# Wide queries, 129-column key-value products, split key weights, and tile keys that are spread without transfers, in a four-layer attention kernel

## The chip, the cores and the metric

The kernel runs on one core of a Trainium2 chip. The core has five engines that run their own instruction streams and wait for each other through semaphores: TensorE (PE, matrix products into PSUM, with PEld for its weight loads), VectorE (DVE), ScalarE (ACT), GpSimd (POOL) and SyncE (SP), which here only issues transfers. Sixteen DMA engines move data. The metric is the device time of one execution in microseconds, less is better, as a median over several runs.

## The reference: what is computed

A stream `x` of 2048 tokens by 512 values (bfloat16) passes through four residual layers. Layers 1 and 3 are linear attention (A), layers 2 and 4 are attention over a sliding window of 256 tokens (B); both have 32 heads of 16 values.

```
phi = lambda t: jnp.where(t > 0, t + 1, jnp.exp(t)) + 1e-6
pq, pk = phi(q), phi(k)
kv = jnp.einsum("bhsd,bhse->bhde", pk, v)
z = jnp.einsum("bhsd->bhd", pk)
num = jnp.einsum("bhqd,bhde->bhqe", pq, kv)
den = jnp.einsum("bhqd,bhd->bhq", pq, z)[..., None] + 1e-6
o = num / den
...
x = x + _A_ref(_layernorm(x, axis=-1), A_wqkv, A_wo)
x = x + _B_ref(_layernorm(x, axis=-1), B_wqkv, B_wo)
x = x + _A_ref(_layernorm(x, axis=-1), A_wqkv, A_wo)
x = x + _B_ref(_layernorm(x, axis=-1), B_wqkv, B_wo)
```

B is softmax attention in which token i sees tokens i-255 to i. Layer A couples all tokens: `kv` and `z` are sums over the whole sequence, so no output of layer 3 exists before the last key and value of layer 3.

## The kernel before

Tokens are worked on in 16 tiles of 128. Everything stays in SBUF; only weights, `x` and the result pass through HBM. The work falls into five stretches, and neighbouring layers overlap in them:

- **Keys of layer 1** (`layer_a_keys`): per tile the normalisation (`norm`: statistics and `xn` on DVE, a power on POOL), the transpose into `XQ` (by PE for the first five tiles, by DMA for the others), the keys `k`, their feature map `phi` (`E` on ACT, `E1` and `phi` on DVE; for some tiles `R` on ACT and `mx` on DVE in place of `phi`), and a running product of keys and normalised input (`g`, L501).
- **First barrier** (`barrier(1)`): `kv`, its masked copy `pqd`, the four products `M` with the output weights, the denominators (`den`, `rec`, `spread`, and `pqd` or `sc` with `pm`).
- **Middle of layer 2** (`middle(2)`): for each tile the end of layer 1 (`aout`, `res`, a second `norm`, transposed into `xT`), the projections of layer 2 (`bq`, `bk`, `bv`), scores, exponentials on ACT (L686, L801, L721, L754), masks on DVE and POOL, values (`pv`), the end of layer 2 and the keys and values of layer 3.
- **Second barrier** (`barrier(2)`): the same for layer 3. Here `kv` is summed from keys and values tile by tile (`a_kv`).
- **Middle of layer 4** (`middle(3)`, called the last layer here) with the write of the result.

The queries of A (`a_q`, L434 of the form ps<-XQ,wA) are not tied to a place: they fill PE wherever it would wait. One call handles a tile: two groups of eight products of 128x128 by 128 columns, then `phi` into the same columns of `XQ`.

In `a_kv` each tile takes four products of 128 columns (L477) and four of one column with a vector of ones (L480), which give `z`. The result has values on partitions and keys in columns, which is the side from which the product `M` (L547) reads it.

The denominators come from five steps of four products each; the first of the five adds the 1e-6 through a small product of constants (`eps`, `ones`).

The keys of layer B stand in `kB` in a form with every second entry zero, because 64 keys and 64 zeros are interleaved for two heads. In most tiles `bk` is evicted once (`bke`, L627 on ACT, L628 on DVE) into a zeroed buffer, from which two transfers (`kd`, L636) write the even and the odd partitions into `kB`. For tile 0 alone (`NEAR`) two evictions with a per-partition factor of one or zero (`kz`, L624) write `kB` directly. `kB` has four slots; tile t uses slot t modulo 4.

The order of the work is written out. The program lists its operations with their data dependencies; `place` reads from a packed string, `TABLE`, the order of all operations, the engine of each one that may run on two, and the PSUM bank of each tile. Each engine plays its instructions in that order, and a semaphore wait is put where a dependency crosses engines. So an instruction that waits holds up all that stand behind it on its engine. All input and transposing transfers, `kd` and `vd`, and a part of the output transfers are issued by SP in one queue.

Of the kernel before, what the change touches and what calls it, by code (L numbers as in the profile page):

```python
# [11 lines left out]
P = 128  # L12
# [3 lines left out]
T = 16  # L16
# [207 lines left out]
NEAR = (0,)  # L224
# [11 lines left out]
class Plan:  # L236
# [51 lines left out]
    def setup(self):  # L288
# [10 lines left out]
        seq += [xs(0, 1), w("wAk", "wA", "A_wqkv", 512, 1024), xs(1, 2), w("wAq", "wA", "A_wqkv", 0, 512), xs(2, 4), xs(4, 6), xs(6, 8), xs(8, 12)]  # L299
# [4 lines left out]
        for i, (n, f, b, r) in enumerate(seq):  # L304

            begun.append(self.load(n, f, b, r, key + i if i < 8 else 100.5 + 0.5 * i, begun[i - 4:i - 3] if i >= 7 else []))
# [59 lines left out]
    def norm(self, t, key, xn_slot, out, wr, by_pe, po=None, near=False):  # L366

        K = self
        xn, name = (lambda: K.vA[:, t, :], ("vA", t)) if xn_slot is None else (lambda: K.xn[:, xn_slot, :], ("xn", xn_slot))
# [40 lines left out]
    def tok(self, name, t, lhs, rhs, rd, key, whole=False):  # L410
# [5 lines left out]
        for h in range(2):  # L416
# [5 lines left out]
            self.pe(name, put, key - 0.001 * h, 2, 512, rd=rd, ps=[ps])  # L422
# [16 lines left out]
    def phi(self, ps, out, wr, key, ring, near=False):  # L439
# [3 lines left out]
        view = lambda x: x if len(out().shape) == 2 else x.rearrange("p (f n) -> p f n", f=4)  # L443
        self.on("ACT", "E", lambda e: e.activation(K.tE[:, s, :], K.ps(ps), ACT.Exp, bias=0.0), key, act(512), wr=[("tE", s)], ps=[ps])  # L444
        if near:
            self.on("ACT", "R", lambda e: e.activation(out(), view(K.ps(ps)), ACT.Identity, bias=K.one[:]), key + 0.005, act(512), rd=[("one",)], wr=wr, ps=[ps])
# [3 lines left out]
        else:  # L450
            self.on("DVE", "phi", lambda e: e.scalar_tensor_tensor(out(), view(K.ps(ps)), 1.0 + 1e-6, view(K.tE[:, s, :]), ALU.add, ALU.max), key + 0.02, dve(512), rd=[("tE", s)], wr=wr, ps=[ps])

    def a_k(self, t, key):
        K = self
        xT = lambda c: K.XQ[:, c, t * P:(t + 1) * P]
        ps = self.tok("k", t, xT, lambda c: K.wA[:, c, 512:1024], [("XQ", t), ("wAk",)], key)
        self.phi(ps, lambda: K.pk[:, t, :], [("pk", t)], key + 0.1, 0)

    def a_v(self, t, key):
# [3 lines left out]
        self.copy("ve", ps, lambda: K.vA[:, t, :], lambda: K.ps(ps), key + 0.1, 512, wr=[("vA", t)] + ([("kS", 0), ("kS", 1)] if t == 2 else []))  # L463

    def a_q(self, t, key, near=False):
        K = self
        ps = self.feat("q", t, lambda c, f: K.wA[:, c, f * P:(f + 1) * P], lambda c: K.XQ[:, c, t * P:(t + 1) * P], [("XQ", t), ("wAq",)], key)
        self.phi(ps, lambda: K.XQ[:, :, t * P:(t + 1) * P], [("XQ", t)], key + 0.1, 1, near)

    def a_kv(self, t, kv, z, key):  # L470
        K = self

        def put(e):
            m = None
            for f in range(4):
                fs = slice(f * P, (f + 1) * P)
# [692 lines left out]
```

## Time and profile before

| what | value |
|---|---|
| median of three runs | 409.82 us (409.52 to 409.96) |
| the profiled execution | 409.61 us, of which 407.9 us are the span from the first to the last instruction |
| granted TensorE clock | 1.00 |
| PE, DVE, ACT, POOL busy | 385.7, 347.8, 349.4, 131.3 us |

A busy time is the time in which at least one instruction of the engine was under way. For PE it includes the tail of some 0.17 us in which the last product of a group drains, so the rate of a product is better read from the chain of work, where a group counts only until the next one begins. A row of the chain or of the timeline has the start, the length, the engine, the tiles, the line of the program and how many instructions are in it; what stands in square brackets is the idle time of the engine ahead of it and what ended it. A row of the groups has the busy time, the mean duration of one instruction in ns, and the idle time ahead of it. Rows of the windows have, after the length, the busy time of PE, PEld, DVE, ACT and POOL with the count of instructions.

### The profile page before, as it was taken

How to read it: one execution, taken by the hardware profiler on the slowest of the kernel's cores; microseconds unless marked ns; L12 is line 12 of the kernel's file. 1: busy time of each engine (PE TensorE's matmuls, PEld its weight loads, DVE VectorE, ACT ScalarE, POOL GpSimd, SP SyncE). 2: the span in 40 equal slices, each digit the busy share in tenths (PEclk: the TensorE clock that was granted, in tenths of full speed). 3: DMA queues.
4: the chain of work that ended last, by engine and by line, in shares of the span. 5: the costliest groups of instructions: out<-in, count | busy, mean ns of one | idle time of the engine just before them, and what ended most of it. 6: DMA issues, size and time to landing. Idle time of an engine off the chain costs nothing.

```text
span 407.9 us, 17534 instructions
## 1 busy us (share of the span) xinstructions
PE 385.7 (95%) x7667; PEld 261.3 (64%) x7742; DVE 347.8 (85%) x807; ACT 349.4 (86%) x441; POOL 131.3 (32%) x221
## 2 busy tenths in 40 slices
PE   8999999998999999999999999999999989998996
PEld 3754776776575567565667677686756756666664
DVE  7998899999989999888788779998998688856865
ACT  3753679998999999999997258999999999999992
POOL 5668542211430241432512302230305234510340
PEclk9999999999999999999999999999999999999999
DMA  7567024523354444453232000344315534442551
GB/s 251 117 152 232 15 56 107 119 69 81 80 80 106 71 101 104 92 112 91 56 50 62 14 2 2 102 114 107 94 42 106 90 90 104 81 99 70 136 134 54
DMA packets 66788, 37.19 MB, mean 91 GB/s; under 512 B 47640, under 2 KB 62104, under 8 KB 66712
## 3 DMA queue, kind: packets, MB, share of 16 engines
q1 hardware_dynamic: 66320, 35.02, 36.7%
q8 instruction: 61, 1.00, 1.1%
q0 software_dynamic: 384, 1.05, 0.8%
q14 instruction: 15, 0.12, 0.1%
q10 hardware_dynamic: 8, 0.00, 0.0%
HBM read 6.29 MB, written 2.10 MB: 21 GB/s over the span
## 4 chain that ended last, share of the span: by engine, by line
PE 52%; ACT 31%; DVE 9%; issue 4%; DMA 2%; POOL 1%; POOLq 0%; DVEq 0%
ACT pb L686 20%; PE ps L420 18%; PE ps L434 15%; PE ps L822 6%; ACT vp L686 5%; PE ps L676 4%; PE ps L501 3%; ACT pb L801 3%; DVE stats L374 1%; DVE pb L694 1%; DVE xres L604 1%; ACT tE L444 1%; PE ps L792 1%; DMA XQ<-xn 1%; ACT pb L754 1%
## 5 line engine op out<-in xcount | busy, mean ns | idle before, releaser
L686 ACT ACTIVATE pb<-ps 128x1024 bf16<-128x1024 f32 (+2 forms) x216 | 199.0, 1019 | 6.2 <-PE ps L676 5.3
L822 PEld LDWEIGHTS ps<-vB,pb 128*128 128x128 bf16 x2560 | 79.0, 96 | 13.3 <-DVE pb L694 2.8
L822 PE MATMUL ps<-vB,pb 128*128 128x34 bf16 x2560 | 84.9, 177 | 0.9 <-DVE xn L381 0.5
L434 PE MATMUL ps<-xT,wBp 128*128 128x128 bf16 x1024 | 69.3, 219 | 1.3 <-DMA xT<-xn 0.8
L434 PEld LDWEIGHTS ps<-xT,wBp 128*128 128x128 bf16 x1024 | 58.9, 98 | 13.7 <-issue 4.0
L772 POOL TENSOR_SCALAR_AFFINE_SELECT pb<-pb 128x1024 bf16<-128x1024 bf16 x35 | 40.1, 1145 | 84.2 <-DVE pb L694 33.8
L379 POOL TENSOR_SCALAR ve<-mv 128x1 f32<-128x1 f32 x63 | 16.6, 264 | 149.1 <-DVE mv L375 146.9
L444 ACT ACTIVATE tE<-ps 128x512 bf16<-128x512 f32 x64 | 38.1, 606 | 25.3 <-PE ps L420 12.5
L676 PE MATMUL ps<-XQ,kB 32*128 32x256 bf16 (+3 forms) x992 | 48.0, 267 | 2.9 <-ACT vp L686 0.5
L604 DVE TENSOR_TENSOR xres<-ps,xres 128x512 bf16<-128x512 f32 x63 | 43.0, 684 | 7.3 <-PE ps L420 6.8
L420 PE MATMUL ps<-wA,XQ 128*128 128x512 bf16 x174 | 45.8, 379 | 3.4 <-DMA XQ<-xn 0.9
L694 DVE TENSOR_TENSOR pb<-pb,tri 128x512 bf16<-128x512 bf16 (+1 forms) x108 | 43.6, 417 | 2.7 <-ACT pb L686 2.0
L374 DVE BATCH_NORM_STATS2 stats<-xres 128x6 f32<-128x512 bf16 x64 | 43.5, 683 | 2.5 <-DMA xres<-in_A_x_dram 1.9
L380 POOL TENSOR_TENSOR rs<-ve,negh 128x1 f32<-128x1 f32 x64 | 39.5, 616 | 7.7 <-DVE ve L377 2.4
L801 ACT ACTIVATE pb<-ps 128x1024 bf16<-128x1024 f32 x42 | 41.3, 1058 | 0.5 <-PE ps L792 0.4
L434 PE MATMUL ps<-XQ,wA 128*128 128x128 bf16 x512 | 35.5, 219 | 0.2 <-issue 0.2
L434 PEld LDWEIGHTS ps<-XQ,wA 128*128 128x128 bf16 x512 | 30.8, 98 | 6.6 <-DVE xres L604 0.2
L420 PE MATMUL ps<-wBv,xT 128*128 128x512 bf16 x107 | 30.6, 380 | 2.8 <-issue 1.6
L420 PE MATMUL ps<-M,XQ 128*128 128x512 bf16 x112 | 30.5, 380 | 2.0 <-DVE XQ L591 0.5
L420 PE MATMUL ps<-wBo,oT 128*128 128x512 bf16 x109 | 29.8, 380 | 1.8 <-issue 0.8
L676 PEld LDWEIGHTS ps<-XQ,kB 32*128 32x128 bf16 x992 | 14.9, 92 | 25.7 <-ACT pb L686 8.4
L834 DVE RECIPROCAL rc<-ps 128x16 f32<-128x16 f32 x64 | 16.2, 253 | 14.4 <-PE ps L822 13.9
(126 smaller groups left out, 557.4 us busy)
## 6 DMA issues: line engine op xcount, KB each, us to landing
vB<-vS SPq DMA_DIRECT2D x64, 136.0 KB, 2.5
kB<-vp SPq DMA_DIRECT2D x60, 128.0 KB, 2.2
wA<-in_A_wqkv_dram SPq DMA_DIRECT2D x3, 512.0 KB, 4.5
xres<-in_A_x_dram SPq DMA_DIRECT2D x2, 512.0 KB, 5.6
pb<-in_B_wqkv_dram SPq DMA_DIRECT2D x1, 1024.0 KB, 5.5
out_dram<-xres POOLq DMA_DIRECT2D x8, 128.0 KB, 3.2
out_dram<-xres SPq DMA_DIRECT2D x7, 128.0 KB, 3.0
xres<-in_A_x_dram SPq DMA_DIRECT2D x3, 256.0 KB, 4.8
```

The lines of the kernel that those rows point to most:

```text
L374: self.on("DVE", "stats", lambda e: e.bn_stats(K.stats[:, t, :], x()), key, dve(512), rd=rd, wr=[("stats", t)], **held)
L380: self.pow = self.on("POOL", "pow", lambda e: e.tensor_tensor(K.rs[:, t, :], K.ve[:, t, :], K.negh[:], ALU.pow), key + 0.03, (640, 690), r ...
L420: m = e.matmul(K.ps(ps), lhs(c), rhs(c), start=c == 0 and not whole, stop=c == 3)
L434: m = e.matmul(K.ps(ps)[:, f * P:(f + 1) * P], w(c, f), xT(c), start=c == 0, stop=c == 3)
L444: self.on("ACT", "E", lambda e: e.activation(K.tE[:, s, :], K.ps(ps), ACT.Exp, bias=0.0), key, act(512), wr=[("tE", s)], ps=[ps])
L604: self.on("DVE", "res", lambda e: e.tensor_tensor(K.xres[:, t, :], K.ps(po), K.xres[:, t, :], ALU.add), key, dve(512), rd=[("xres", t)], w ...
L676: m = e.matmul(K.ps(ps[gq])[:, ns * i:ns * i + ns], K.kB[rows, j % 4, 2 * f + b, :, :], K.XQ[rows, f, q:q + ns], start=True, stop=True, ti ...
L686: return e.activation(out(2 * h, 2, ns), i, ACT.Exp, bias=0.0, scale=0.25)
L694: return e.tensor_tensor(x, x, K.tri[:, 0, sh:64].unsqueeze(1).unsqueeze(1).to_broadcast([P, 4, n, 64 - sh]), ALU.mult)
L772: return e.affine_select(out=x, in_=x, compare_op=ALU.is_ge, fill=0.0, base=-2, pattern=[[0, 16], [-2, 64]], channel_multiplier=1)
L801: return e.activation(far(h), i, ACT.Exp, bias=0.0, scale=0.25)
L822: m = e.matmul(K.ps(ps)[:, 34 * u:34 * u + 34], K.P((b // 2) % rp)[:, gq, f, o:o + P], K.vB[:, (b // 2) % 4, b % 2, r, :], start=i == 0, s ...
```

## The change

Five edits and a new table:

1. **Wide queries.** `a_q` handles a pair of tiles: each of the two PSUM tiles takes two of the four feature blocks, with products of 256 columns that span both tiles. Per pair that is 16 products of 256 columns for 32 of 128. The feature map then writes two feature blocks of both tiles, and may do so only when everything that reads the two tiles of `XQ` has been done.
2. **129-column key-value products.** The rows of `vA` grow from 512 to 516 columns; behind every 128 columns of values stands a one, written by `unit`, two POOL instructions in all. `a_kv` takes four products of 129 columns, whose last column is `z`; the products with the vector of ones are gone. Keys now lie on partitions, so the masked `kv` goes through four PE transposes and a copy before `M`. `kvm` and `zs` become two halves each. The rows of `vA` in layer 1, from which the transposing transfers read, start at multiples of 1032 bytes, where it was 1024.
3. **Denominators.** For the last three of four groups the product with the constants goes, and a DVE instruction `de` adds 1e-6 in PSUM.
4. **Split key weights.** The key weights arrive in two transfers of 256 KB, and each half of the first product waits for its own.
5. **Keys of tiles 8 to 15 of the last layer** take the path of tile 0: two evictions `kz`, no `bke`, no `kd`.

The new `TABLE`, unpacked, has 2564 operations for 2559. By engine, before and after: PE 866 and 867, ACT 440 and 441, DVE 806 and 820, POOL 217 and 220, SP 230 and 216. All 16 new `kz` stand on DVE, as the eight `bke` in their place did. The copy of the transposed `kv` stands on DVE. Of the masks `mf` of layer 2, five move from DVE to POOL and one the other way before its last tiles. In the second barrier the transposed `xn` of the last tile is evicted by DVE in place of ACT, three queries' steps (two `E`, one `R`) stand ahead of the first eviction of `xT`, and one eviction of `xT` moves from ACT to DVE. On SP the output of one early tile stands behind the two last halves of the result. Otherwise the new order resembles the old one, with neighbours exchanged.

```diff
-NEAR = (0,)
+NEAR = {2: (0,), 3: (0, 8, 9, 10, 11, 12, 13, 14, 15)}
...
+        def wk(h):
+            return ("wAk%d" % h, lambda e: e.dma_start(K.wA[:, 2 * h:2 * h + 2, 512:1024], K.A_wqkv.rearrange("(k p) c -> p k c", p=P)[:, 2 * h:2 * h + 2, 512:1024]), 262144, [("wAk", h)])
...
-        self.copy("ve", ps, lambda: K.vA[:, t, :], lambda: K.ps(ps), key + 0.1, 512, wr=[("vA", t)] + ([("kS", 0), ("kS", 1)] if t == 2 else []))
...
+    def a_q(self, u, keys, near):
...
+        own = [("XQ", 2 * u), ("XQ", 2 * u + 1)]
+        wide = lambda t: slice(256 * (t // 2), 256 * (t // 2) + 256)
...
+                    f = 2 * (t % 2) + h
+                    for c in range(4):
+                        m = e.matmul(K.ps(ps)[:, 256 * h:256 * h + 256], K.wA[:, c, f * P:(f + 1) * P], xT(c), start=c == 0, stop=c == 3)
...
+        held = [o for x in own for o in self.g.r[x]]
...
+            self.phi(tiles[d], out, wr, keys[d] + 0.1, 1, t in near, after=held)
+
+    def unit(self, a, b, more, key):
...
+        self.g.add("unit", {"POOL": (300, 360), "DVE": dve(4 * (b - a))}, lambda e, eng: e.memset(x(), 1.0), key, wr=[("vA", t) for t in range(a, b)] + more)
...
-                e.matmul(K.ps(kv)[:, fs], K.vA[:, t, fs], K.pk[:, t, fs], start=t == 0 and f == 0, stop=t == T - 1, skip_group_check=True)
...
-                m = e.matmul(K.ps(z)[:, f:f + 1], K.pk[:, t, fs], K.ones[:, 0:1], start=t == 0 and f == 0, stop=t == T - 1, skip_group_check=True)
+                m = e.matmul(K.ps((kv, z)[f // 2])[:, 129 * (f % 2):129 * (f % 2) + 129], K.pk[:, t, f * P:(f + 1) * P], K.vA[:, t, 129 * f:129 * f + 129], start=t == 0 and f % 2 == 0, stop=t == T - 1, skip_group_check=True)
...
+        if late:
+            for h, x in enumerate((kv, z)):
...
+                self.on("DVE", "kvm", lambda e, h=h, two=two: e.tensor_tensor(K.oT[:, 0, 2 * h:2 * h + 2, :], two()[:, :, 0:P], K.bmask[:].unsqueeze(1).to_broadcast([P, 2, P]), ALU.mult), key - 2, dve(256), rd=[("bmask",)], wr=[("kvT", h)] + ([] if h else [("oT", 0)]), ps=[x])
...
+            self.transpose("T", lambda: K.oT[:, 0, :, :].rearrange("p f n -> p (f n)"), lambda: K.pqd[:], [("oT", 0), ("kvT", 0), ("kvT", 1)], [("pqd",)], key - 2, True)
...
-                for i in range(5):
+                for i in range(1 if G else 0, 5):
...
+            if G:
+                self.on("DVE", "de", lambda e, ps=ps: e.tensor_scalar(K.ps(ps)[:, 0:P], K.ps(ps)[:, 0:P], 1e-6, None, op0=ALU.add), k + 0.05, dve(128), ps=[ps])
...
-        if t in NEAR:
+        if t in NEAR[2 + (self.rp == 4)]:
...
+ROW = D + 4
...
-            sb("vp", [2 * T, D]); sb("kB", [4, 8, 64, 2]); sb("vB", [4, 2, 16, 34]); sb("pb", [3, 4, 4, 704])
+            sb("vp", [T * (ROW + D)]); sb("kB", [4, 8, 64, 2]); sb("vB", [4, 2, 16, 34]); sb("pb", [3, 4, 4, 704])
```

More of the change, by code (lines that the diff above doesn't have):

```diff
@@ L437, in feat, with phi @@
         return ps
-    def phi(self, ps, out, wr, key, ring, near=False):
+    def phi(self, ps, out, wr, key, ring, near=False, after=()):
         K = self
@@ L450, in phi @@
         else:
[L451 removed]
+            self.on("DVE", "phi", lambda e: e.scalar_tensor_tensor(out(), view(K.ps(ps)), 1.0 + 1e-6, view(K.tE[:, s, :]), ALU.add, ALU.max), key + 0.02, dve(512), rd=[("tE", s)], wr=wr, ps=[ps], after=after)
     def a_k(self, t, key):
@@ L949, in middle @@
         if not last:
+            self.unit(0, LATE, [("kS", 0), ("kS", 1)], base + 14)
             for j in range(LATE):
```

178 lines of the change are left out of this document (98 added, 80 removed).

## The prediction

> **What bounds the kernel now.** I read the page first for the engines and the chain of work, then the busy time by stretches, then the chain piece by piece where the change touches it.
>
> ```profile
> PE 385.7 (95%) x7667; PEld 261.3 (64%) x7742; DVE 347.8 (85%) x807; ACT 349.4 (86%) x441; POOL 131.3 (32%) x221
> ...
> PE 52%; ACT 31%; DVE 9%; issue 4%; DMA 2%; POOL 1%; POOLq 0%; DVEq 0%
> ```
>
> PE holds half of the chain and ACT a third, so the bound changes from stretch to stretch. The windows show where (columns: length, then PE, PEld, DVE, ACT, POOL busy):
>
> ```profile
> 7.00:57.00 50.00, 49.45 (x522) 30.33 (x527) 46.37 (x115) 28.09 (x50) 32.57 (x63) 1.00 0.49 130
> 57.00:90.00 33.00, 31.90 (x614) 23.43 (x610) 30.83 (x71) 31.63 (x39) 7.76 (x18) 1.00 0.41 101
> 90.00:117.00 27.00, 24.62 (x555) 16.79 (x557) 26.68 (x63) 25.52 (x31) 8.70 (x12) 1.00 0.41 80
> 117.00:213.00 96.00, 92.12 (x1895) 60.11 (x1917) 83.08 (x193) 94.13 (x109) 28.61 (x45) 1.00 0.40 86
> 213.00:249.00 36.00, 34.36 (x622) 25.59 (x629) 29.07 (x68) 20.38 (x37) 6.90 (x11) 1.00 0.12 25
> 249.00:276.00 27.00, 26.69 (x504) 19.90 (x507) 26.55 (x63) 25.68 (x35) 8.41 (x15) 1.00 0.35 87
> 276.00:320.00 44.00, 42.48 (x968) 29.79 (x975) 38.75 (x86) 43.30 (x49) 12.14 (x18) 1.00 0.40 88
> 320.00:395.00 75.00, 69.38 (x1790) 46.30 (x1797) 55.28 (x127) 74.14 (x87) 20.68 (x24) 1.00 0.41 96
> ```
>
> Up to 57 us PE works without a gap (49.45 of 50). In layer 2 ACT, PE and DVE are all nearly full, with DVE ahead at 90 to 117 (26.68 of 27) and ACT from 117 on (94.13 of 96). At the second barrier ACT idles for 15.6 us while PE goes on (34.36 of 36). From 276 to 395 ACT has 117.4 of 119 us and cannot be sped up by anything that leaves its work alone; DVE has 25 us to spare there. So PE work is worth its time before 57 and around the barrier, and little elsewhere.
>
> **The change part by part.** The rates of PE stand in the chain:
>
> ```profile
> 24.39 0.86 PE ps L501 x4
> 47.22 0.89 PE ps L434 x16
> 53.06 0.22 PE ps L395 x4
> 239.74 0.24 PE ps L477 x4
> 239.99 0.08 PE ps L480 x4
> 240.53 0.39 PE ps L563 x20
> ```
>
> *Wide queries.* Sixteen products of 128 columns take 0.89 us (56 ns each), four of 512 columns 0.86 us (215 ns each). On the line between these two a product of 256 columns is 109 ns, so a tile costs 8 x 109 = 0.87 us for 0.89: 0.02 us saved, 0.7 us over 32 tiles. Bounds: nothing saved, and 32 x 8 x 56 ns = 14 us if only the count mattered, which the 215 ns of the 512-column row exclude. About 12 tiles' worth lies before 57 us and as much around the barrier. In return a pair's feature map waits for the last reader of both tiles; the cover is that a query's place is free, since it fills PE.
>
> A rule of the Trainium skill would make far more of this edit: "TensorE: Matmul & The Clock Gate", section Back-to-back issue gap, gives about 81 ns for a product of 128 columns in a real stream with its weight load and 131 ns for 512. An estimate by that page, with 98 ns between the two, is 512 x 81 - 256 x 98 = 16 us of PE saved. The trace does not agree: 56 and 215 ns.
>
> *Key-value products.* Four one-column products take 0.08 us per tile, 16 x 0.08 = 1.3 us of PE, nearly all between 227 and 241, where the chain runs through PE. The 129th column is nothing. Four transposes come in, 0.22 us on PE, and their copy. The path behind the last `kv` is what the barrier waits for:
>
> ```profile
> L543 DVE TENSOR_TENSOR pqd<-ps,bmask 128x512 bf16<-128x512 f32 x2 | 1.4, 687 | 0.0
> L544 DVE TENSOR_TENSOR zs<-hot,ps 128x128 bf16<-128x128 bf16 x2 | 0.6, 288 | 1.1 <-PE ps L480 0.6 <-PE ps L524 0.5
> L402 DVE COPY XQ<-ps 128x512 bf16<-128x512 bf16 x1 | 0.4, 408 | 0.0
> L835 DVE TENSOR_TENSOR o<-ps,rc 128x256 bf16<-128x256 f32 x64 | 26.7, 419 | 1.5
> L628 DVE CAST vp<-ps 128x512 bf16<-128x512 f32 x25 | 18.3, 731 | 3.2 <-PE ps L434 3.1
> L624 ACT ACTIVATE kB<-ps,par 128x512 bf16<-128x512 f32 x4 | 3.4, 840 | 0.3 <-PE ps L434 0.3
> L773 DVE TENSOR_TENSOR pb<-pb,tri 128x1024 bf16<-128x1024 bf16 x15 | 10.0, 683 | 0.0
> L375 DVE BATCH_NORM_AGGREGATE mv<-stats 128x2 f32<-128x6 f32 x64 | 10.5, 170 | 0.6
> ```
>
> Before: `zs` 0.29 and `kvm` 0.69, together 0.98 us. After: two halves of `kvm` at 0.42 (the 256-column row of `div`), the transposes 0.22 with some 0.2 us to drain, the copy 0.41: 1.67 us, with `zs` beside the transposes. So `M` comes 0.7 us later behind the same last `kv`. The eviction of the last tile's `xn` by DVE gives 0.2 us back, and the last `kv` products come earlier. The cover is query work: the chain there has no idle PE, so a later `M` lets queries go first. Without that cover it costs the 0.7 us.
>
> *Denominators.* Twenty products take 0.39 us, so four less save 0.08 us six times, 0.5 us of PE. Six `de` come in: as dear as the 128-column row of `zs`, 0.29 us, with 0.17 (a statistics merge) as the least I would grant; 1.7 us of DVE, two of them before 117 us where DVE is full (0.6 us). There five masks at 0.68 us go to POOL and one comes back: 2.7 us less on DVE. POOL is a third busy.
>
> *Keys of tiles 8 to 15.* Eight `bke` of 0.73 us become sixteen `kz` on DVE. Price: 0.73 each, the row that reads the same PSUM tile and writes the same stride; ends 0.68 (`kvm`) and 0.84 (the `kz` on ACT). DVE gains 5.8 us where 25 are idle, so I take nothing, and 5.8 us if that cover is not where it is needed. Sixteen transfers go:
>
> ```profile
> kB<-vp SPq DMA_DIRECT2D x60, 128.0 KB, 2.2
> ...
> L676 PEld LDWEIGHTS ps<-XQ,kB 32*128 32x128 bf16 x992 | 14.9, 92 | 25.7 <-ACT pb L686 8.4 <-ACT pb L801 1.8 <-DVE o L835 1.4
> ```
>
> The 2.2 us to landing are not among what the scores wait for, so their end is worth nothing by itself. SP's queue becomes shorter for the transposes behind them. What is new is that `kz` writes a slot of `kB` that the scores of four tiles earlier read: that wait leaves SP and stands in DVE's order, ahead of masks, divisions and sums.
>
> *Split weights and `unit`.* The first key product begins here:
>
> ```profile
> 6.10 0.60 ACT L402 ACTIVATE XQ<-ps 128x512 bf16<-128x512 bf16 x1 [2.80 <-PE ps L395]
> 6.82 0.13 PEld L420 LDWEIGHTS ps<-wA,XQ 128*128 128x128 bf16 x2
> ```
>
> Its input is ready at 6.70, so earlier weights gain at most 0.1 us; one more issue on SP may cost as much further back. I take zero. `unit` is two small POOL instructions, zero.
>
> *The end.* SP issues one early output behind the two halves of the last tile:
>
> ```profile
> 403.88 0.81 SPq L878 DMA_DIRECT2D out_dram<-xres  x2
> ...
> 405.27 0.54 POOL L942 DMA_DIRECT2D out_dram<-xres  x1 [8.32 <-DVE xres L604]
> ```
>
> It would begin at 404.7, before the last one on POOL at 405.27, which has the same size and ends the program either way: zero, and 0.6 us at most if SP's lands last.
>
> *The new order at the barrier.* ACT's way to the first exponential of the last layer:
>
> ```profile
> 246.62 0.62 ACT L407 ACTIVATE tE<-ps 128x512 bf16<-128x512 f32 x1
> 248.76 0.60 ACT L402 ACTIVATE xT<-ps 128x512 bf16<-128x512 bf16 x1 [1.53 <-PE ps L395]
> 256.24 1.94 ACT L721 ACTIVATE pb<-ps 128x1024 bf16<-128x1024 f32 x2 [0.16 <-PE ps L712]
> ```
>
> Two `E` and an `R` move ahead of the eviction at 248.76, into the idle 1.53 us, and one eviction of `xT` leaves ACT: some 2 us less ACT work between 248.76 and 256.24, one `bke` of 0.8 more. But ACT only just waited for PE there (0.16 us), and PE's work between the same two points shrinks by one query group and one denominator group that move ahead of it. So PE decides, and PE's saving is what counts.
>
> **Sum**, against the profiled execution's 409.61 us (the median of 409.82 is 0.2 higher): before 57 us, queries and a denominator, -0.3; 57 to 117, DVE's 2.7 - 0.6 = 2.1 us less, of which ACT can take up no more than its idle 2.9 us and PE is as full, so a quarter, -0.5; 117 to 213 nothing; barrier, -1.3 (ones) - 0.3 (queries) + 0.2 (transposes), -1.4, of which the later `M` takes back 0.2; last layer -0.1 for two denominators; the end nothing. Together -2.1: 407.5 us.
>
> **The rivals.**
>
> *A, slower: DVE in the last layer.* The second `kz` of each of eight tiles lies on the path, and DVE holds masks back. For it: the chain passes such an eviction already, and the new wait stands in DVE's order:
>
> ```profile
> 308.90 0.73 DVE vp L628
> ```
>
> Against it: 25 us of idle DVE. It decides once the stretch from 276 to 395 shows ACT waiting for PE behind DVE for more than 2 us. Price 8 x 0.73 = 5.8: 413.3 us.
>
> *B, no change.* The barrier's path is latency, not PE: `M` comes 0.7 us later with ACT waiting for it, and takes 0.7 of the 1.4 and the query part: 407.5 + 1.6 = 409.1 us and above. For it: ACT idles 15.6 us there, so something is late. Against it: PE's 34.36 of 36.
>
> *C, more.* The order fills ACT's idle time at the barrier: the 2 us of ACT work that move forward count in full: 405.5 us. For it: ACT bounds all that follows. Against it: the 0.16 us.
>
> *D, weight loads.* These take longer than the products they feed:
>
> ```profile
> L434 PEld LDWEIGHTS ps<-XQ,wA 128*128 128x128 bf16 x512 | 30.8, 98 | 6.6 <-DVE xres L604 0.2 <-ACT pb L686 0.2 <-DVE rc L834 0.2
> ```
>
> If PE paid them, 512 products at 98 ns would become 256 at 109, a saving of 22 us, three quarters of it where PE bounds: 393 us. The 0.89 us for sixteen speak against it. The rule of "TensorE: Matmul & The Clock Gate" quoted above points this way.
>
> **How the numbers follow.** No change means within 0.2% (0.8 us), about what the runs can tell apart. My sum (406.3 to 409.0): 0.45. C: 0.17. D: 0.02. B (409.0 to 410.6): 0.12. A: 0.17, and 0.07 for smaller losses at the barrier or from paired queries that hold `phi` (410.6 to 412). Faster 0.64, same 0.12, slower 0.24. The range from 404.2 to 412.0 leaves out D, the lower end of C and the upper half of A, some 0.15; the likeliest case's own range is 406.3 to 409.0.
>
> **What would show it.** In the profile after: 8 products of 256 columns in 0.87 us; no L480; PE busy some 2 us less; the first exponential of the last layer 1.5 to 2 us earlier; ACT as full between there and the end as before; DVE fuller by 6 us and its waits for PE shorter by as much. It is wrong if PE or ACT wait for `kz`, if the first exponential is not earlier, or if the tail behind the last exponential grows by an output transfer that SP now issues last.

## The result, and the profile after

The changed kernel is slower by a third of a per cent: 411.16 us (median of 9 runs, 410.57 to 411.68) against 409.74 us for the kernel before (9 runs beside it), ratio 1.0033, interval 1.0021 to 1.0045. A second set of runs gave 411.09 us and 1.0034 (1.0022 to 1.0046). The forecast was 407.5 us; the time lies in its range and on the wrong side of no change.

The page of the changed kernel, busy times and chain of work; then its windows over the same stretches as before:

```profile
PE 385.2 (94%) x7327; PEld 255.9 (62%) x7402; DVE 353.8 (86%) x821; ACT 350.5 (86%) x442; POOL 133.2 (33%) x224
...
PE 65%; ACT 19%; DVE 9%; issue 5%; POOL 1%; DMA 1%; POOLq 0%
```

```profile
7.00:57.00 50.00, 49.51 (x416) 28.74 (x421) 45.25 (x114) 27.75 (x50) 33.03 (x65) 1.00 0.50 132
57.00:90.00 33.00, 31.90 (x592) 22.78 (x597) 32.09 (x70) 31.07 (x37) 10.57 (x20) 1.00 0.45 104
90.00:117.00 27.00, 25.70 (x542) 16.94 (x543) 25.47 (x63) 25.58 (x31) 7.44 (x12) 1.00 0.32 81
117.00:213.00 96.00, 91.43 (x1866) 59.20 (x1886) 83.57 (x192) 93.75 (x108) 29.80 (x45) 1.00 0.39 84
213.00:249.00 36.00, 35.22 (x527) 24.30 (x532) 30.27 (x76) 23.74 (x43) 9.20 (x15) 1.00 0.14 28
249.00:276.00 27.00, 26.52 (x480) 19.18 (x485) 26.30 (x61) 24.85 (x31) 4.96 (x12) 1.00 0.38 87
276.00:320.00 44.00, 40.98 (x913) 28.53 (x923) 36.79 (x87) 42.61 (x49) 13.18 (x18) 1.00 0.32 79
320.00:395.00 75.00, 67.40 (x1737) 46.24 (x1748) 61.36 (x134) 72.86 (x84) 19.82 (x26) 1.00 0.34 72
```

ACT does 3.4 us more in the 36 us around the barrier (23.74 for 20.38), as the order meant, and 2.0 us less from 276 to 395 (115.5 for 117.4): there it is kept waiting. It holds 19% of the chain where it had 31%, and PE 65% for 52%. DVE is busy 6.0 us longer, the forecast's figure. The chain, at the places that the forecast named (lines moved: L483 queries, L506 `kv`, L398 transposes, L405 the copy, L581 `M`, L662 `kz`, L859 `pv`):

```profile
10.73 0.44 PE ps L483 x4
...
237.15 1.18 PE ps L506 x20
238.34 0.87 PE ps L483 x8
239.21 0.39 PE ps L398 x4
239.60 0.02 issue
239.62 0.44 DVE pqd L405
240.06 0.27 issue
240.33 0.59 PE ps L581 x2
...
339.33 0.77 DVE kB L662
340.10 0.02 issue
340.13 0.81 DVE kB L662
340.94 0.05 issue
340.98 1.37 PE ps L859 x48
```

Queries of 256 columns run at 109 ns each, as estimated. At 339 us the two `kz` of a tile stand on the chain one behind the other, and PE's value products start when the second ends. The timeline has the first exponential of the last layer, and the groups the new DVE instructions:

```profile
255.18 2.96 ACT L758 ACTIVATE pb<-ps 128x1024 bf16<-128x1024 f32 x3
```

```profile
L662 DVE TENSOR_SCALAR kB<-ps,par 128x512 bf16<-128x512 f32 x16 | 12.7, 795 | 2.8 <-PE ps L437 2.0 <-PE ps L713 0.5
L602 DVE TENSOR_SCALAR ps<-ps 128x128 f32<-128x128 f32 x6 | 1.7, 289 | 0.0
L573 DVE TENSOR_TENSOR oT<-ps,bmask 128x256 bf16<-128x256 f32 x2 | 0.8, 420 | 0.5 <-PE ps L506 0.5
```

The first exponential came at 255.18 (before 256.24), `de` takes 0.29, the halves 0.42 and `kz` 0.80 us (I took 0.73).

**Three marks.** The window layers have 312 exponentials. I use the start of the 131st (in layer 2), the 186th (early in the last layer) and the 306th (near its end) as marks, and compare what lies between them. The windows between marks 1 and 2 and between 2 and 3, of the kernel before and of the changed one (second profile):

```profile
199.10:285.83 86.73, 84.13 (x1560) 59.88 (x1576) 75.15 (x175) 69.61 (x98) 21.32 (x34) 1.00 0.25 58
285.83:395.73 109.90, 102.93 (x2574) 70.50 (x2588) 86.18 (x195) 108.34 (x127) 33.36 (x43) 1.00 0.41 93
```

```profile
198.71:285.80 87.09, 84.67 (x1415) 58.55 (x1431) 76.92 (x183) 71.16 (x100) 17.76 (x32) 1.00 0.24 56
285.80:397.38 111.58, 101.17 (x2533) 69.90 (x2551) 91.64 (x201) 108.91 (x127) 32.62 (x43) 1.00 0.34 75
```

**The start differs by chance.** PE's first products run at half rate, 427 ns for 512 columns in place of 216, and the change comes at another moment in each profile, 4.5 to 7.2 us into the span, whatever the kernel. The chain of the kernel before, then of the changed one:

```profile
5.20 0.65 PE ps L277 x3
```

```profile
5.27 1.28 PE ps L277 x3
```

In the programs that are alike up to tile 8 of the last layer, a change at 7.1 us put mark 1 at 198.78 and one at 5.4 us at 198.10, so each us costs about 0.4; `e14_moved`, with 5.8 us and 198.50, shows that single profiles scatter by some 0.3 us besides. The section What's actually happening of the Trainium skill's "TensorE: Matmul & The Clock Gate" has such a gate at half rate with a window that runs freely, which the scatter here agrees with. Medians average it out; single profiles are compared below by their stretches.

### The profile page after: what moved, and what is told of

It is laid out like the page before. It is cut to its first block, busy times and chain, and to the rows that moved or that the text cites. A ratio compares the mean times of both kernels' runs of the same rounds, so it can differ in the third digit from the quotient of the medians.

```text
span 409.7 us, 16880 instructions
## 1 busy us (share of the span) xinstructions
PE 385.2 (94%) x7327; PEld 255.9 (62%) x7402; DVE 353.8 (86%) x821; ACT 350.5 (86%) x442; POOL 133.2 (33%) x224
## 4 chain that ended last, share of the span: by engine, by line
PE 65%; ACT 19%; DVE 9%; issue 5%; POOL 1%; DMA 1%; POOLq 0%
PE ps L423 22%; PE ps L859 12%; ACT pb L723 11%; PE ps L437 10%; PE ps L713 6%; PE ps L483 5%; PE ps L527 3%; ACT pb L838 3%; ACT vp L723 2%; DVE kB L662 2%; PE ps L829 1%; DVE xres L641 1%; ACT tE L447 1%; PE ps L1124 1%; PE ps L506 1%
## 5 line engine op out<-in xcount | busy, mean ns | idle before, releaser
L859 PEld LDWEIGHTS ps<-vB,pb 128*128 128x128 bf16 x2560 | 78.8, 96 | 13.7 <-issue 2.1
L859 PE MATMUL ps<-vB,pb 128*128 128x34 bf16 x2560 | 84.3, 177 | 1.1 <-POOL pb L809 0.3
L809 POOL TENSOR_SCALAR_AFFINE_SELECT pb<-pb 128x1024 bf16<-128x1024 bf16 x38 | 43.7, 1150 | 97.0 <-DVE pb L731 29.9
L423 PE MATMUL ps<-wA,XQ 128*128 128x512 bf16 x175 | 44.4, 379 | 1.5 <-issue 0.3
L483 PE MATMUL ps<-XQ,wA 128*128 128x256 bf16 x256 | 33.6, 273 | 0.9 <-ACT pb L723 0.5
L423 PE MATMUL ps<-wBo,oT 128*128 128x512 bf16 x101 | 28.0, 379 | 3.5 <-issue 1.1
L483 PEld LDWEIGHTS ps<-XQ,wA 128*128 128x128 bf16 x256 | 23.5, 98 | 8.1 <-ACT pb L723 0.9
```

The source lines that it names most:

```text
L423: m = e.matmul(K.ps(ps), lhs(c), rhs(c), start=c == 0 and not whole, stop=c == 3)
L483: m = e.matmul(K.ps(ps)[:, 256 * h:256 * h + 256], K.wA[:, c, f * P:(f + 1) * P], xT(c), start=c == 0, stop=c == 3)
L809: return e.affine_select(out=x, in_=x, compare_op=ALU.is_ge, fill=0.0, base=-2, pattern=[[0, 16], [-2, 64]], channel_multiplier=1)
L859: m = e.matmul(K.ps(ps)[:, 34 * u:34 * u + 34], K.P((b // 2) % rp)[:, gq, f, o:o + P], K.vB[:, (b // 2) % 4, b % 2, r, :], start=i == 0, s ...
```

## The experiments

Runs of one group shared the runs of the kernel before (medians 409.64 to 410.19 us in five groups). Where an edit adds or drops operations, the table is written anew with all others in their places.

The column of the rate change has the start of the first product of 512 columns at the full rate in the run's profile.

| run | median | ratio to before | rate change | mark 1 | 1 to 2 | 2 to 3 |
|---|---|---|---|---|---|---|
| before | 409.74 | 1 | 5.0 | 199.10 | 86.73 | 109.90 |
| changed | 411.16 | 1.0033 | 7.1 | 198.78 | 87.09 | 111.71 |
| after_again | 411.09 | 1.0034 | 6.8 | 198.71 | 87.09 | 111.58 |
| e1_transfers | 409.94 | 1.0001 (0.9991 to 1.0011) | 6.6 | 198.47 | 87.09 | 110.45 |
| e9_later | 410.39 | 1.0003 (0.9990 to 1.0015) | 6.7 | 198.78 | 87.08 | 110.64 |
| e10_one | 410.13 | 1.0010 (0.9997 to 1.0023) | 7.1 | 198.77 | 87.08 | 112.86 |
| e10_again | 410.22 | 1.0017 (0.9995 to 1.0040) | 5.4 | 198.10 | 87.06 | 110.29 |
| e2b_eight | 412.04 | 1.0048 (1.0034 to 1.0062) | 4.9 | 198.76 | 86.53 | 111.87 |
| e3_narrow | 411.69 | 1.0041 (1.0026 to 1.0055) | 5.3 | 198.57 | 87.27 | 111.54 |
| e4_ones | 412.86 | 1.0067 (1.0052 to 1.0083) | 5.8 | 198.19 | 88.60 | 112.59 |
| e5_oldkv | 412.79 | 1.0073 (1.0059 to 1.0087) | 5.3 | 199.01 | 88.43 | 112.26 |
| e8_eps | 410.84 | 1.0030 (1.0016 to 1.0045) | 5.8 | 198.28 | 87.11 | 111.81 |
| e11_few | 410.02 | 1.0000 (0.9984 to 1.0015) | 5.0 | 198.96 | 85.51 | 110.16 |
| e12_parts | 411.47 | 1.0051 (1.0035 to 1.0066) | 4.5 | 199.89 | 86.84 | 110.48 |
| e13_parts_eps | 410.59 | 1.0023 (1.0011 to 1.0035) | 7.2 | 200.00 | 86.65 | 111.81 |
| e14_moved | 411.23 | 1.0027 (1.0016 to 1.0038) | 5.8 | 198.50 | 87.02 | 111.92 |
| e15_both | 411.88 | 1.0038 (1.0024 to 1.0052) | 5.8 | 197.94 | 87.06 | 111.99 |

(All but the ratios in us.) Three more runs, e2_twice, e6_masks and e7_old_order, are told at their places. The changed kernel itself, run once more:

> The changed kernel itself beside these two, so that all stand against the same runs of the kernel before: 411.2 us, give or take 0.3, and a profile with another moment at which TensorE's clock goes up (it was at 7.1 us in its first profile and 5.0 us in that of the kernel before, worth about 1.0 us). By both theories the stretch between the exponentials at 326 and 384 us is 2.5 us longer than before again.

411.09 us, with the rate change at 6.8 us. From the 226th exponential to the 286th it takes 54.8 us (326.17 to 380.95) where the kernel before takes 52.7 (326.86 to 379.54): 2.1 longer.

### The keys on DVE

```diff
-NEAR = {2: (0,), 3: (0, 8, 9, 10, 11, 12, 13, 14, 15)}
+NEAR = {2: (0,), 3: (0,)}
```

> The changed kernel with tiles 8 to 15 of the last layer back on one strided eviction (bke) and two transfers (kd) each, in the places of the order where the two kz stood. Theory K (the sixteen kz on DVE are on the path): in the changed kernel each step from the exponential at 326 us to that at 384 us of the last layer is later against the kernel before, by 2.5 us in sum; with the transfers back this goes, so 411.2 - 2.5 = 408.7 us, and the kernel is faster than the one before. Theory O (the new order, not kz, loses the time, since the keys are needed some 13 us after they are written): 411.2 us, give or take 0.3.

409.94 us: level with the kernel before, 1.2 us under the changed one. Nothing changed up to mark 2; from 2 to 3 it is 110.45 us for 111.6. So the sixteen `kz` cost 1.2 us in that place, half of what theory K gave them, and they are not all of the loss: without them the kernel is level, not 2.1 us faster. In this run a transpose stood behind two key transfers on SP; moving these back in the order (`e9_later`) gave nothing more:

> The run e1_transfers once more, with the two key transfers of tiles 8 to 15 placed 22 places later in the order, behind the transposes that SP had to hold back in that run (its chain shows a transpose of xn from 323.2 to 327.3 us behind two such transfers). Theory K (the transfers cost nothing if they stand where nobody queues behind them): 409.9 - 1.0 = 408.9 us, below the kernel before. Theory O (the order loses the time elsewhere): 409.9 us, give or take 0.3.

410.39 us, ratio 1.0003: that transpose was not what kept it from falling under the kernel before.

What of `kz` costs, its length or its new wait for `kB`, is told apart by one instruction for both halves:

```diff
+            wide = lambda x: x.to_broadcast([P, 512, 2])
+            self.on("DVE", "kz", lambda e: e.tensor_tensor(K.kB[:, r].rearrange("p b n a -> p (b n) a"), wide(K.ps(pk).unsqueeze(2)), wide(K.par2[:].unsqueeze(1)), ALU.mult), ...)
```

> The changed kernel with both zero-padded halves of tiles 8 to 15 written by one DVE instruction (the PSUM tile, each column twice, times the pair of masks, 1,024 columns) in the place of the first kz. By the rows two kz hold DVE and the key product's bank for 1.6 us; one instruction of 1,024 columns from PSUM should take about 1.2 (twice the 0.6 of a 512-column eviction). Theory K (time of DVE and bank): a quarter of the 1.2 us that kz costs comes back, 411.2 - 0.3 = 410.9 us. Theory W (the wait of kz for the last readers of its slot is what costs, not its duration): 411.2 us.

> The run e10_one once more, since its first profile caught a drop of TensorE's clock at 317.6 us that cost 2.5 us there: 410.1 us, give or take 0.3, and, without the drop, the stretches from 303 to 326 and from 326 to 381 us about 0.1 and 1.0 us shorter than in the changed kernel (23.2 and 54.8).

410.13 and 410.22 us. The instruction takes 1.22 us where two took 1.6, so DVE and the bank are held 0.37 us less per tile, 2.9 us in all:

```profile
L660 DVE TENSOR_TENSOR kB<-ps,par 128x1024 bf16<-128x1024 f32 x8 | 9.8, 1223 | 2.6 <-PE ps L437 2.0 <-PE ps L717 0.6
```

About 1.0 of the 1.2 us comes back, against the 0.3 that theory K expected in proportion. The wait for the slot is as it was, so theory W falls: the length counts. An eviction of 1.22 us costs next to nothing in this place and two of 0.80 one behind the other cost 1.2; whether the two count by their length alone was not told apart. The waits of the changed kernel from 276 to 396 us (us in total, times, longest) name who waits: value products and scores, for the bank in which the key product lay.

```profile
PEld ps L859 <- DVE kB L662: 1.5, 4, 0.7
PEld ps L713 <- DVE kB L662: 1.0, 1, 1.0
PE ps L713 <- DVE kB L662: 0.9, 1, 0.9
```

The same from the other side, the kernel before with the eviction made twice:

```diff
-                    e.tensor_copy(keys(), ...)
+                    [e.tensor_copy(x, ...) for x in [keys(), aside()][:2 if t >= 8 and end else 1]][-1]
```

> The kernel before with the eight bke of tiles 8 to 15 of the last layer made twice, in the last layer alone (the run e2_twice had doubled those of layer 2 as well, so that it wrote over weights still in use, and its time stands for up to sixteen doubled evictions). DVE is held 5.8 us longer and the key product's PSUM bank 0.73 us longer per tile; result and order as before. Theory K (DVE time and bank in the last layer are on the path): between 1.2 us, what giving the transfers back won in the changed kernel, and 5.8: 411 to 415.6 us. Theory O (25 idle us of DVE cover it): 409.8 us, give or take 0.3.

412.04 us, 2.1 more, and the stretch from mark 2 to 3 grows by 1.97 us for 5.7 us of added DVE time. Theory O falls in the old order too: DVE's idle time there covers two thirds of an added eviction, not all. (An earlier form of this run doubled the evictions of layer 2 as well, up to sixteen, and wrote over weights still in use; it took 414.53 us, ratio 1.0109.)

> The kernel before, with each of the eight bke of tiles 8 to 15 of the last layer made twice: the second one reads the same PSUM tile and writes to an unused place, so DVE is held 8 x 0.73 = 5.8 us longer there and the key product's PSUM bank as much, with every transfer, the order and the result as they were. Theory K: 409.7 plus at least 2 us, at most 5.8: 411.7 to 415.5. Theory O (DVE has 25 us to spare there): 409.7 us, give or take 0.3.

### The parts at the barrier

Each wide product made as two narrow ones, and each 129-column product as one of 128 columns and one of a single column:

```diff
-                        m = e.matmul(K.ps(ps)[:, 256 * h:256 * h + 256], ..., xT(c), ...)
+                        for n in range(2):
+                            m = e.matmul(K.ps(ps)[:, 256 * h + P * n:256 * h + P * n + P], ..., xT(c)[:, P * n:P * n + P], ...)
```

> The changed kernel with each query product of 256 columns made as two of 128 columns in the same place, same order, same result. By the rows of the trace (four of 256 in 0.44 us, sixteen of 128 in 0.89): 32 x 0.02 = 0.6 us more of PE in all, of which about half where PE bounds: 411.2 + 0.3 = 411.5 us. If the count of products mattered, as rival D had it, 256 more products at some 50 to 60 ns would add 14 us of PE and about 10 us to the time: 421 us.

```diff
-                m = e.matmul(..., K.vA[:, t, 129 * f:129 * f + 129], ...)
+                e.matmul(..., K.vA[:, t, 129 * f:129 * f + P], ...)
+            for f in range(4):
+                m = e.matmul(..., K.vA[:, t, 129 * f + P:129 * f + 129], ...)
```

> The changed kernel with each 129-column key-value product made as one of 128 columns and one of a single column against the ones of the same row, same order, same result: the one-column products of the kernel before come back (64 of them, 1.3 us of PE by their row), while the halves, the transposes and the denominators stay as changed. If PE bounds the barrier, as my prediction had it: 411.2 + 1.3 = 412.5 us. If the barrier is latency, as rival B had it: 411.2 us.

411.69 us: wide queries are worth the small gain that the rows gave them (0.5 us by the medians, whose intervals overlap, where 0.3 was expected); rival D is out. The Trainium skill's "TensorE: Matmul & The Clock Gate", section Back-to-back issue gap, gives 81 ns for products of 128 columns in a real stream; with 0.5 us for 256 more products this run does not bear that out. 412.86 us: the one-column products are worth 1.4 (by the ratios) to 1.7 us in the changed order, and the stretch from mark 1 to 2 grows by 1.5. So PE does bound that stretch, up to the first exponential of the last layer: that comes 57.93 us behind mark 1 for 56.41. With the whole old path, whose `M` comes 0.7 us earlier:

```diff
-                m = e.matmul(..., K.pk[:, t, f * P:(f + 1) * P], K.vA[:, t, 129 * f:129 * f + 129], ...)
+                e.matmul(K.ps(kv)..., K.vA[:, t, 129 * f:129 * f + P], K.pk[:, t, f * P:(f + 1) * P], ...)
+            for f in range(4):
+                m = e.matmul(K.ps(z)[:, f:f + 1], K.pk[:, t, f * P:(f + 1) * P], K.ones[:, 0:1], ...)
...
-            for h, x in enumerate((kv, z)):
-                ... two kvm, two zs
-            self.transpose("T", ...)
+            ... one kvm, one zs
```

> The changed kernel with the whole key-value path of the kernel before: value rows as weights, four one-column products against the ones, one kvm of 512 columns and one zs, no transposes and no copy behind them; the rest of the order as changed. It differs from the run e4_ones (412.9 us) by the halves, the transposes and the copy, which make M 0.7 us later. If that later M is on the path: 412.9 - 0.7 = 412.2 us or less. If query work covers it, as my sum had it but for 0.2: 412.9 - 0.2 = 412.7 us. If the ones cost PE nothing after all and e4 was slow for its split groups: 411.2 us.

412.79 us, level with 412.86; the stretch from mark 1 to 2 differs by 0.17 us. The halves, transposes and copy cost at most some 0.2 us in the changed order: query work covers them, as the forecast had it, and rival B's mechanism is not there.

Then the same parts in the old order. First the one-column products of 14 tiles left out of the kernel before:

```diff
-            for f in range(4):
+            for f in range(4 if t in (0, T - 1) else 0):
                 m = e.matmul(K.ps(z)[:, f:f + 1], ...)
```

> The kernel before with the one-column products left out for 14 of the 16 tiles of the second linear layer (the sums of keys then hold two tiles only, so the denominators of that layer are not the reference's): 56 x 20 ns = 1.1 us less of PE and nothing else, in the old order. My prediction counts PE's time at the barrier in full: 409.9 - 1.1 = 408.8 us. Rival B (latency, or the gain is given back where ScalarE bounds the last layer): 409.9 us, give or take 0.3.

The medians do not settle it: 410.02 us, runs from 408.84 to 411.92. The profiled execution took 408.84 us with its rate change at the same moment as that of the kernel before (409.61), and its stretch from mark 1 to 2 is 85.51 us, 1.2 less. In the stretch of this one profile, the fastest of the twelve runs, PE's saving counts in full; whether the time keeps it, these runs leave open.

Then all parts but wide queries and `kz`, in the order, engines and banks of the kernel before:

> The parts of the change without wide queries and without kz for tiles 8 to 15 (129-column products, halves and transposes, denominators with de, split weights, unit), in the order, engines and banks of the kernel before, the new instructions set in beside those that they belong to. Theory P (the parts are worth what my sum gave them, and the changed order gives it back): 409.8 less the 1.6 us that the run e4_ones found for the one-column products, so 408.2 us, some tenths less if the denominators count. Theory Q (the parts themselves eat the gain: later M, six de): 409.8 us or above.

417.4 us, ratio 1.0182. It answers nothing, because of where I put the memset of the ones: it stood in POOL's queue behind the landing of key transfers, and the masks stood behind it.

```profile
L477 POOL MEMSET vp<- 128x44 bf16 (+2 forms) x3 | 0.6, 193 | 11.6 <-DMA kB<-vp 11.5
```

Mended:

```diff
-            self.unit(0, LATE, ...)
             for j in range(LATE):
                 self.a_v(j, ...)
+                self.unit(j, j + 1, [], base + 14)
```

> The run e7_old_order mended: there the memset of the ones (unit) for the last five value tiles waited on POOL for key transfers, 7 us in which POOL's queue stood, masks and all; here each of these five is a small DVE instruction behind the eviction of its value tile. All else as there: 129-column products, halves and transposes, six de, split weights, narrow queries, transfers for tiles 8 to 15, in the order of the kernel before. Theory P (the parts win what the forecast gave them, the new order loses it): 409.9 less 1.1 to 1.6, so 408.3 to 408.8 us. Theory Q (the parts themselves take the gain back): 409.9 us or above.

> The same as e12_parts without the six de: the small number is added by TensorE as in the kernel before. If de costs what my sum said (0.6 us on DVE before 117 us against 0.5 on PE in all): within 0.3 us of e12_parts. If de is a loss: 0.5 us or more below it.

The second of these has the edit of `e8_eps` (below) as well. 411.47 and 410.59 us. Theory Q holds in the old order: mark 1 to 2 takes 86.84 us, 1.3 more than with the ones merely left out. The transposes stand next in PE's order there, and PE waits for the halves of `kvm` (the waits of `e12_parts` from 238 to 257 us):

```profile
PE ps L398 <- DVE oT L551: 0.7, 1, 0.7
```

With the 0.4 us of the transposes behind it that is most of the 1.3: the new path takes back what the ones win. The six `de` cost 0.9 us more, all of it ahead of mark 1: with `de` mark 1 comes at 199.89 after a rate change at 4.5 us, without it at 200.00 after one at 7.2, so some 0.9 us later at an equal start. In the changed order `de` shows no such price:

```diff
-                for i in range(1 if G else 0, 5):
+                for i in range(5):
...
-            if G:
-                self.on("DVE", "de", ...)
```

> The changed kernel with the small number of the denominators added by TensorE again, as in the kernel before (a fifth round of four products in each group), and the six additions (de) on DVE gone; all else as changed. If the six de (1.7 us of DVE, two of them where DVE is full, and each between a denominator and its reciprocal) are the loss that the one-column products' gain went into: 411.2 - 1.0 = 410.2 us or less. If they are as cheap as my sum had them (0.6 us on DVE against 0.5 on PE): 411.2 us, give or take 0.3.

410.84 us, ratio 1.0030 for 1.0033: level.

### The order

Counted in the written order of PE's queue, from the operation that feeds mark 1 to the one that feeds mark 2, the changed kernel has 26 query operations for 24, 5 transposes for 4, 24 `pv` for 23 and 11 `bout` for 10, and of all else the same number. By the chain's rows (0.44, 0.22, 0.59, 0.43) that is 2.1 us of PE more, against 1.3 for the ones and some 0.4 for narrower queries and denominators. The difference, +0.4, is what the stretch shows, 87.09 for 86.73. But the two query operations stood ahead of mark 1 before, and the stretch from the 100th to the 131st exponential is 0.7 us shorter without them (32.20 us for 32.90); the `pv` and the `bout` stood behind mark 2. Work that is carried over a mark looks like a loss on one side and a gain on the other.

Two other exponentials are better marks: at the 157th, the first of the last layer, and at the 201st both orders have done the same work on PE, but for the four new transposes and one operation (one `bq` less at the 157th, one `pv` less at the 201st). The windows between them, of the kernel before and of `e10_again`:

```profile
256.24:302.93 46.69, 45.88 (x936) 32.20 (x943) 43.42 (x96) 45.29 (x52) 9.80 (x15) 1.00 0.36 92
```

```profile
254.49:302.33 47.84, 46.16 (x874) 30.46 (x871) 43.17 (x98) 45.67 (x53) 9.81 (x16) 1.00 0.35 86
```

The same work takes 1.15 us longer. Every profile in the changed order has 47.8 to 47.9 us here (or 49.3 in the two runs below): with the transfers back (`e1_transfers`, 47.85), without `de` (`e8_eps`, 47.85), with the old key-value path (`e5_oldkv`, 47.87), with narrow products (`e3_narrow`, 47.89). Every profile in the old order that was compared has 46.7 to 47.1, whether it has the parts (`e12_parts`, 46.87; `e13_parts_eps`, 47.07) or a lead of 1.4 us at the 157th exponential (`e11_few`, 46.69). So none of these parts costs this time. The order does, or the pairing of the query tiles, which the changed order has in every run and the old one in none: no run separates these two.

The loss falls between the 176th and the 186th exponential, which take 11.03 us for 9.03; up to the 176th the changed order still gains 0.9 us, from two `pv` and two query operations that it puts off. Ahead of the scores of these the changed order has 6 `pv` for 3, two query operations for none, 3 `bout` for 2 and 3 `bv` for 4. Whether work can go back behind the scores was tried with two query operations and one `bout` (1.3 us), on top of `e10_one`:

> The run e10_one with three pieces of TensorE work put later in the order, as the kernel before has them: the two query operations q57 and q58 (0.87 us) from ahead of the score operation s93 to behind it, and bout35 (0.43 us) from ahead of s92 to ahead of bout36. In the changed order the stretch from the exponential at 275 us to that at 286 us is 11.0 us with TensorE busy for 10.9 of it, in the kernel before 9.0 us with ScalarE full. Theory E (work pulled ahead of the scores keeps ScalarE waiting there and spends the barrier's saving): the stretch 1.3 us shorter, and the time up to that much below 410.1: 409.0 us. Theory S (TensorE's sum decides, whatever stands first): the stretch shorter, the next one longer by the same, 410.1 us.

> e14_moved without the six de, the small number added by TensorE again. The run e8_eps stood 0.2 to 0.3 us below the changed kernel, which is no more than its scatter; e13_parts_eps stood 0.9 us below e12_parts. If de costs in this order too: 0.3 to 0.9 us below e14_moved. If not: level with it.

411.23 and 411.88 us, 1.0 and 1.7 above `e10_again`. The stretch to mark 2 stays at 87.0, and the 17.2 us from there to the 201st exponential become 18.7. That does not decide theory E: of the three pieces only the `bout` (0.43 us) stood ahead of the operation that feeds mark 2, the two query operations stood right behind it. The chain of `e14_moved` says why the next scores do not start earlier without the `bout`:

```profile
281.77 0.36 PE ps L717 x8
282.13 0.02 issue
282.15 1.95 ACT vp L727 x2
284.10 0.05 issue
284.15 0.43 PE ps L717 x8
```

They (L717) wait for the banks that two exponentials hold. So these runs show where the time is lost, and that it goes with the order or the pairing; which exchange of the order costs it was not shown.

The masks of layer 2 put back on DVE, at the places that they have on POOL:

> The changed kernel with the masks of layer 2 on the engines of before (five mf of the first tiles back on DVE, one back on POOL), order and result as changed: 2.7 us more on DVE before 117 us. My prediction gave that relief, with the two de, 0.5 us: so 411.2 + 0.5 = 411.7 us or a little more. Rival: while POOL works on masks DVE's own mask multiplications are slower (28 of them took 11.56 us in the stretch before 199 us of the kernel before, and 12.61 in the changed one), so the move gave nothing: 411.2 us, give or take 0.3.

416.52 us, ratio 1.0153, and no answer to the question: one mask at its POOL place stands in DVE's queue ahead of evictions and waits there for an exponential, PE goes idle for 2.0 us, and its clock falls:

```profile
85.00:87.00 2.00, 0.00 (x1) 0.01 (x1) 1.96 (x4) 1.95 (x3) 0.00 (x0) 1.00 0.51 136
87.00:89.00 2.00, 2.00 (x24) 1.77 (x25) 1.52 (x4) 0.00 (x0) 0.00 (x0) 0.84 0.24 48
89.20:91.40 2.20, 2.20 (x48) 1.91 (x47) 0.69 (x1) 0.58 (x1) 0.00 (x0) 0.50 0.33 67
```

No version came out below the kernel before; `e1_transfers`, `e9_later` and `e10_one` are level with it.

## Why the prediction was wrong

Set against its own sum, by marks at which both orders have done the same work, with the start netted out (`e10_again`, alike up to the keys of tile 8, for the first two rows; 0.15 us for its rate change):

| stretch | forecast | measured |
|---|---|---|
| to the 157th exponential, the first of the last layer | -2.0 (-0.3, -0.5, -1.4 and +0.2) | 254.49 - 256.24 - 0.15 = -1.90 |
| 157th to 201st | 0 | 47.84 - 46.69 = +1.15 |
| 201st to mark 3 | -0.1 | 94.4 to 94.5 for 92.8: +1.6 to +1.7 |
| behind mark 3 | 0 | 12.1 to 12.4 for 12.2: 0 to +0.3 |

**Keys of tiles 8 to 15: the first step that failed.** "DVE gains 5.8 us where 25 are idle, so I take nothing": the gain in busy time was right (6.0 with the rest) and the nothing was wrong: 1.2 us by `e1_transfers`, and 5.7 us more DVE work in the kernel before cost 2.1. Idle time summed over 119 us says nothing of the moment when a bank is waited for. Rival A named the mechanism and the place, and asked for 2 us of ACT waiting behind DVE; its price, every second `kz` in full, was four to five times too high. My 0.17 for it was too low, the more so since the chain of before already passed such an eviction.

**The order behind the first exponential: the second.** I called it one that "resembles the old one" and put it at nothing there. From the 157th to the 201st exponential it takes 1.15 us more for the same work, and so spends more than half of what the barrier wins. I had taken ACT to bound all that follows; in this stretch it is idle for 2.2 us where it was 1.4, and busy 0.4 us longer. Whether an exchange of neighbours or the pairing of queries does it stays open. In the old order the parts win nothing for another reason, PE's wait for the halves ahead of the transposes (`e12_parts`), which is rival B's latency. None of the tried orders had the saving without a price.

**Up to the first exponential the sum held**, -1.9 for -2.0 (other pairs of profiles give -1.2 to -2.0). Ahead of the first exponential of layer 2 it is -0.1 (59.95 for 59.90, less the 0.15) where -0.3 was forecast, from there to the 100th -0.3 (105.96 for 106.30) where -0.5 was, from the 100th to the 157th -1.5 (88.58 for 90.04) where -1.2 was. The sizes at the barrier were right too: the ones 1.4 to 1.7 (`e4_ones`), the later `M` at most 0.2 (`e5_oldkv`), wide queries 0.5 over all (`e3_narrow`). The reason for the -0.5 was not: of the masks that leave DVE only two, net, stand before 117 us (5 instructions of 128x1024 there before, 3 after), not the four of the 2.7 us, and DVE's busy time from 57 to 117 us stays at 57.5. That this term came out near is luck.

**The last layer behind the 201st exponential** is 0.3 to 0.7 us longer even without the second `kz` (93.3 us in `e1_transfers`, 93.5 in `e9_later`, 93.1 in `e10_again`, for 92.8). But `e11_few`, which is the kernel before in that stretch, has 93.1, so much of this may be scatter.

That 411.16 us lies in the piece from 410.6 to 412, to which I gave 0.07, is luck in part: it was kept for losses at the barrier or from paired queries, and 1.2 us of the loss is `kz`, which was priced elsewhere.

**Of what I said would show it**: 256 columns at 109 ns and no one-column products, yes; the first exponential 1.1 us earlier in a profile whose start cost 0.8, so nearly 2, yes; ACT as full behind it, no (115.5 for 117.4); DVE 6 us fuller, yes; and PE waits for `kz`, which I had named as the sign of being wrong. PE's busy time (385.2 for 385.7) tells nothing, as it depends on how much of the half-rate start it holds. Split weights and the output on SP show no price of their own, but no run takes them out.

## What to carry to other kernels

An engine's idle time in a stretch covers added work only if nobody waits for what the work holds: before an eviction is made longer, look who takes its PSUM bank next, and how many operations later. A saving on the bounding engine is worth what the order leaves of it: count the operations between the same two marks in both orders, not only those that the edit names, and choose marks at which both have done the same work. And where several profiles of one kernel exist, compare stretches between fixed events, since their starts differ by chance.

## What the hardware showed that I had not expected

A pause of PE of 1.5 to 2 us can halve its clock within 1.5 us of its end. In the first profile of `e10_one` PE stood still from 315.28 to 316.75 us, and then (windows):

```profile
317.60:319.50 1.90, 1.90 (x25) 1.59 (x23) 0.83 (x2) 1.53 (x2) 1.75 (x3) 0.51 0.66 155
```

Sixteen products that take 0.89 us took 1.64, and the stretch from mark 2 to 3 was 2.6 us longer than in `e10_again`, the same program (112.86 for 110.29). The Trainium skill's "TensorE: Matmul & The Clock Gate", section What's actually happening, has the rate fall after an idle window of about 3.4 us; here pauses of 1.5 and 2.0 us were enough. A third pause, 2.7 us from 207.2 us on in `e7_old_order`, was followed by a clock of 0.50 as well, and two of 1.05 us (`e14_moved` and `e15_both`) by none; in `e13_parts_eps` the clock was at 0.50 from 399.7 us without a pause above 1 us ahead of it. So the length of a pause is not the whole rule, and what else decides these runs do not show.

A mask multiplication on DVE is slower while POOL works on a mask: between 60 and 220 us the 59 of 512 columns took 417 ns on average before and 445 after, where more of POOL's masks fall beside them.

```profile
L694 DVE TENSOR_TENSOR pb<-pb,tri 128x512 bf16<-128x512 bf16 x59 | 23.9, 417 | 1.9 <-ACT pb L686 1.6
```

```profile
L731 DVE TENSOR_TENSOR pb<-pb,tri 128x512 bf16<-128x512 bf16 x59 | 25.6, 445 | 1.6 <-ACT pb L723 1.6
```

Instruction by instruction, the 52 that run beside no POOL mask in the changed kernel take 410 ns on average, the six that do 760.
